# First loads of a fused attention and FFN kernel: nine transfers on one DMA queue instead of two, and four warm-up matmuls fewer

## The chip, the core and the metric

The kernel runs on one NeuronCore of a Trainium2 chip. The metric is the device time of one execution in microseconds. TensorE (PE) multiplies matrices, with its weight loads shown apart as PEld; VectorE (DVE), ScalarE (ACT) and GpSimd (POOL) work on elements; SyncE (SP) only issues DMAs here. ACT can issue DMAs as well. An instruction that issues a DMA occupies its engine's sequencer for a while; the transfer itself runs on 16 DMA engines and raises a semaphore when it has landed.

## The reference

One input x of 2048 tokens by 640 features goes through two branches, and a gate per token mixes them. Everything is bf16.

```
x = A_x                                          # 1 x 2048 x 640
g = sigmoid((x * gate_w).sum(-1))                # one gate per token
q, k, v = split(x @ wqkv)                        # 32 heads of 20
phi(t) = [softmax(t @ w_phi), softmax(-t @ w_phi)]   # 40 features per head
kv = sum over tokens of phi(k)^T v;  z = sum over tokens of phi(k)
a = (phi(q) kv) / (phi(q) z + 1e-6) @ wo
b = (silu(x @ w_gate) * (x @ w_up)) @ w_down     # hidden width 1728
out = g * a + (1 - g) * b
```

## The kernel before

Tokens are worked in 16 tiles of 128 (number t), features in 5 chunks of 128 (number c). Almost every matmul needs x transposed, with features on the partitions: the tile xT holds it. Tiles 0 to 3 are loaded as they are into xs (`load_x`, items x0 to x3) and transposed by TensorE (`xpose`, items X0 to X3, line 306, with a copy from PSUM to xT on DVE, line 318). Tiles 4 to 15 come through DMA transposes (`load_xt`, items t4 to t15, line 347).

Two lists written out by hand fix the order of everything. `LOADS` is the order in which DMAs are issued:

```
x0 w0 x1 w1 x2 w2 x3 w3 w4 f0 h k0 k1 t4 k2 k3 k4 t5 t6 t7 t8 t9 t10 t11 t12 t13 t14 t15 q0 q1 q2 q3
q4 f1 f2
```

- x0 to x3: x of tiles 0 to 3, 128x640 each. The list `XQ` gives the engine whose queue each is issued on: x0 on SP, x1, x2 and x3 on ACT.
- w0 to w4: the five chunks of the V columns of wqkv, into wvg, 128x640 each. `WQ` puts w0 to w3 on SP and w4 on ACT.
- f0, f1, f2: parts of w_gate and w_up (wg and wu), f0 the first 256 columns of each. h: w_phi (wph).
- k0 to k4: the K columns of wqkv, transposed on the way into wT. q0 to q4: the same for the Q columns. All of f, h, k, t and q are on SP.

A small load of gate_w (gwr) stands ahead of all on ACT. Each engine keeps its own instructions in the order in which they are written, so SP and ACT each run through their share of this list.

`ORDER` is the order of the compute items. The stretch of TensorE that matters here is:

```
H0 .. H8 H12 G X0 H9 H10 U0.0 X1 H11 U1.0 U0.1 U1.1 X2 U2.0 U0.2 U1.2 U2.1 X3 U2.2 U0.3 ...
U2.4 V3 Y F0.1 M1 i3 M0 F0.0 M2 V4 M3 M4 K0 K1 I S0 V6 V5 ...
```

- H (`warm`, line 472): two dummy matmuls of 128x128 on constants. Nothing uses their result. G: gate_w, transposed into a column of wvg.
- Ut.c (`vpart`): V of tile t, the part of chunk c, two matmuls of 320 columns each (line 294), as soon as wvg chunk c and xT of tile t are there. V3, V4 ...: V of a whole tile, ten matmuls.
- F0.1, F0.0: two of the 14 FFN items of the first 512 tokens, ten matmuls of 512 columns each, with wg and wu of f0.
- Y (`w_blocks`): w_phi spread into block-diagonal form (wbd) by POOL and DVE. Mm (`premult`): chunk m of the K weights, multiplied with w_phi ahead of use, from wT chunk m (item km) and wbd.
- K, S, P, E: K projections with exponentials, sums, normalising, and the sums kv. Q, A, B, C, c, O, D later: the same for Q, the output and the final products.

Waits are made by a tracker (`_Tracker.run`): each instruction waits for the semaphores of what it reads and overwrites. Every DMA has a semaphore of its own. PSUM banks are used in pairs, the least recently used first (`next_pair`), so an item that is taken out also moves which pair the following ones use.

Of the kernel before, what the change touches and what calls it, by code (L numbers as in the profile page):

```python
# [6 lines left out]
P = 128  # L7
S_TOK = 2048
D = 640
# [24 lines left out]
"""  # L34

ORDER = """
H0 H1 H2 H3 H4 H5 H6 H7 H8 H12 G X0 H9 H10 U0.0 X1 H11 U1.0 U0.1 U1.1 X2 U2.0 U0.2 U1.2 U2.1
X3 U2.2 U0.3 U1.3 U2.3 U0.4 U1.4 U2.4 V3 Y F0.1 M1 i3 M0 F0.0 M2 V4 M3 M4 K0 K1 I S0 V6 V5 S1 P0
K3 K2 P1 E0 V9 K4 E1 S3 V7 P3 K5 S2 V8 V10 S4 P2 P4 E2 R0 E3 K6 S5 P5 S6 i4 E4 V14 K7 K8 P6 V15 S7
R2 E5 K9 S8 P7 R1 E6 K10 S9 V12 P8 E7 P9 K11 S10 P10 F0.2 R3 F1.2 E8 E9 K12 E10 S11 S12 K14 S14  # L40
# [11 lines left out]
class _Tracker:  # L52
# [90 lines left out]
    def run(self, eng, fn, reads=(), writes=(), dma=False):  # L143
        rkeys = list(dict.fromkeys(k for a in reads for k in self.keys_of(a)))
        wkeys = list(dict.fromkeys(k for a in writes for k in self.keys_of(a)))
        need = {}

        def req(ev, raw):
            if ev is None:
                return  # L150
            s, v = ev
            if s == eng and not dma and (eng == "pe" or not raw):
                return
            if v > need.get(s, 0):
                need[s] = v

        for k in rkeys:
            for kk in self._conflicts(k):
                req(self.lastw[kk], True)
                if k[0] == "psum":  # L160
                    for s, v in self.readers[kk].items():
                        req((s, v), False)
        for k in wkeys:
            for kk in self._conflicts(k):
                req(self.lastw[kk], True)
                for s, v in self.readers[kk].items():
                    req((s, v), False)
        self._wait(eng, need)
        ins = fn()
        if dma:  # L170
            sn = "d%d" % self.ndma
            self.ndma += 1
            self._add_sem(sn)
            inc = 16
        else:
            sn, inc = eng, 1
        ins.then_inc(self.sem[sn], inc)
        self.cnt[sn] += inc
        v = self.cnt[sn]
        snap = dict(self.known[eng])  # L180
        if not dma:
            snap[sn] = max(snap.get(sn, 0), v)
        self.evknow.setdefault(sn, {})[v] = snap
        ev = (sn, v)
        for k in wkeys:
            self.lastw[k] = ev
            self.readers[k] = {}
        for k in rkeys:
            r = self.readers[k]
            if r.get(sn, 0) < v:  # L190
                r[sn] = v
        return ev


def _build(nc, A_x, A_wqkv, A_w_phi, A_wo, B_x, B_w_gate, B_w_up, B_w_down, gate_w, out):
    tr = _Tracker(nc)
    pe, act, dve, pool, sp = nc.tensor, nc.scalar, nc.vector, nc.gpsimd, nc.sync
# [3 lines left out]
    def sb(name, shape, dtype):  # L201
        t = nc.alloc_sbuf_tensor(name, list(shape), dtype)
        tr.reg(t, "sbuf", nc.lookup_mloc(t).addr)
        return t
# [3 lines left out]
    wvg = sb("wvg", [P, 5, D + 2], BF16)  # L208
# [42 lines left out]
    def at(name, shape, dtype, rel):  # L251
        n = mybir.dt.size(dtype)
        for s in shape[1:]:
            n *= s
        assert rel + n <= SLAB, (name, rel + n, SLAB)
        t = nc.alloc_sbuf_tensor_at(name, list(shape), dtype, offset=sbase + rel)
        tr.reg(t, "sbuf", sbase + rel)
        return t
# [4 lines left out]
    xs = at("xs", [P, NPE, D], BF16, 10752)  # L263
# [78 lines left out]
    def dma(e, dst, src, transpose=False):  # L342
        eo = tr.eng[e]

        def fn():
            if transpose:
                return eo.dma_start_transpose(dst, src)
            return eo.dma_start(dst, src)
        rd = [src] if src.tensor.name in tr.base else []
        wr = [dst] if dst.tensor.name in tr.base else []  # L350
        return run(e, fn, rd, wr, dma=True)
# [4 lines left out]
            channel_multiplier=cm), [ap], [ap])  # L356


    XQ = ["sp", "act", "act", "act"]
    WQ = ["sp", "sp", "sp", "sp", "act"]  # L360
    x2 = A_x[0]
    out2 = out[0]

    def load_rows(e, dst, c, c0):
        dma(e, dst, A_wqkv[c * P:(c + 1) * P, c0:c0 + D])

    def load_x(t):
        dma(XQ[t], xs[:, t, :], x2[t * P:(t + 1) * P, :])

    def load_xt(t):  # L370
        dma("sp", xT[:, t, :, :], x2[t * P:(t + 1) * P, :], transpose=True)
# [3 lines left out]
        dma("sp", wu[:, :, c0:c1], B_w_up[:, c0:c1].rearrange("(c p) j -> p c j", p=P))  # L375

    def load_wv(c):
        load_rows(WQ[c], wvg[:, c, 0:D], c, 2 * D)

    dma("act", gwr[0:5, :], bass.AP(gate_w.tensor, gate_w.offset, [[P, 5], [1, P]]))  # L380

# [13 lines left out]
    H0 = [0, 6, 12, 19, 25]  # L395
    H1 = [7, 13, 20, 26, 32]
# [339 lines left out]
    def kv_end():  # L736
# [4 lines left out]
        "H": lambda i: warm(), "i": fills, "X": xpose, "G": gcol, "U": vpart, "V": vtile,  # L741
        "M": lambda m: premult(1, m), "R": lambda m: premult(0, m),
        "K": ktile, "S": knorm, "P": kmul, "p": lambda t: kmul(t, "dve"), "E": kvtile, "x": load_x, "t": load_xt, "w": load_wv, "h": load_phi, "k": lambda m: load_wt(1, m), "q": lambda m: load_wt(0, m),
        "f": lambda i: load_ffn(FCUT[i], FCUT[i + 1]), "L": load_late_weights, "T": tail_weights, "J": gates,
        "Y": w_blocks, "I": kv_begin, "N": kv_end, "Z": z_row,
# [8 lines left out]
def bass_gated_mix__linear_kernel_hedgehog__swiglu_ffn__prompt_kernel(  # L754
    nc: bass.Bass,
    A_x: bass.AP,
    A_wqkv: bass.AP,
    A_w_phi: bass.AP,
    A_wo: bass.AP,
    B_x: bass.AP,  # L760
    B_w_gate: bass.AP,
    B_w_up: bass.AP,
    B_w_down: bass.AP,
    gate_w: bass.AP,
    out: bass.AP,
):
    _build(nc, A_x, A_wqkv, A_w_phi, A_wo, B_x, B_w_gate, B_w_up, B_w_down, gate_w, out)
# [28 lines left out]
```

The softmax here doesn't subtract the row's maximum and nothing guards it: scores larger than these inputs give would overflow.

## Time and profile before

| | |
|---|---|
| median of 4 runs | 289.41 us (289.14 to 290.11) |
| profiled execution | 289.17 us, span in the profile 287.9 us |
| PE busy | 285.0 us, 99% of the span |
| PEld busy | 174.7 us, 61% |
| DVE, ACT, POOL busy | 162.6, 148.1, 160.4 us |
| DMA on SP's queue (q1) | 48190 packets, 20.62 MB |
| DMA on ACT's queue (q10) | 730 packets, 0.68 MB |
| granted TensorE clock | 1.0 |

A line of the timeline reads: start in us, length in us, engine, line of the kernel, operation, tile written <- tiles read, shape, count, and in brackets how long the engine stood idle before it and what released it. SPq and ACTq are the DMA-issuing instructions of those engines: the length is that of the issue, not of the transfer. The landing time of a transfer is counted from the start of its issue. The chain lists the work that ended last, followed back from the end. Matmuls are pipelined and their ends are modelled, so PE looks busy in short waits too; the weight loads (PEld) show these better.

### The profile page before, as it was taken

Reading aid. Unit: us, or ns where it says so; the run is one execution under the profiler, and the core shown is the slowest. Engines: PE = TensorE matmul, PEld = TensorE weight load, DVE = VectorE, ACT = ScalarE, POOL = GpSimd, SP = SyncE. Lnnn points to the kernel's source line nnn. Section 1 sums busy time; section 2 is a strip of 40 time slices with the busy share of each in tenths; the row PEclk is TensorE's granted clock in tenths of the full one; section 3 lists DMA queues with packets and bytes.
Section 4 is the critical chain, followed back from the end, with each engine's and each line's share of the span. In section 5 each row is a group of like instructions: output and inputs, shape, how many; then the busy total and the mean of one; then the engine's idle time right before and its main releaser. Section 6 shows DMA issues by size and latency. Waiting matters only on the chain.

```text
span 287.9 us, 4897 instructions
## 1 busy us (share of the span) xinstructions
PE 285.0 (99%) x1975; PEld 174.7 (61%) x1975; DVE 162.6 (56%) x243; ACT 148.1 (51%) x252; POOL 160.4 (56%) x125
## 2 busy tenths in 40 slices
PE   8999999999999999999999999999999999999997
PEld 6667777575644545557775556675554446656776
DVE  2147748486468987679992385970317799200000
ACT  1478778676775555673445663225575452234112
POOL 8286899789445789835643348350753649601000
PEclk9999999999999999999999999999999999999999
DMA  7987589000010497302293002061020004410101
GB/s 217 174 121 127 102 220 359 14 1 2 2 47 0 100 310 144 69 2 50 50 149 88 10 1 50 2 147 44 2 50 0 2 1 87 89 46 0 49 23 48
DMA packets 48943, 21.62 MB, mean 75 GB/s; under 512 B 39384, under 2 KB 48792, under 8 KB 48920
## 3 DMA queue, kind: packets, MB, share of 16 engines
q1 hardware_dynamic: 48190, 20.62, 31.7%
q10 hardware_dynamic: 730, 0.68, 0.7%
q8 instruction: 16, 0.26, 0.4%
q14 instruction: 7, 0.06, 0.1%
HBM read 9.29 MB, written 2.62 MB: 41 GB/s over the span
## 4 chain that ended last, share of the span: by engine, by line
PE 99%; DVE 0%; issue 0%
PE ps L294 97%; PE ps L472 1%; PE ps L306 1%; DVE osb L724 0%; DVE xT L318 0%
## 5 line engine op out<-in xcount | busy, mean ns | idle before, releaser
L322 POOL TENSOR_TENSOR hT<-hT,us 128x512 bf16<-128x512 bf16 (+1 forms) x56 | 65.6, 1181 | 66.3 <-DVE hT L326 66.0
L326 DVE SCALAR_TENSOR_TENSOR hT<-hT,ps 128x512 bf16<-128x512 bf16 (+1 forms) x56 | 37.6, 684 | 72.9 <-ACT hT L312 60.6
L294 PE MATMUL ps<-xT,wg 128*128 128x512 bf16 x260 | 64.6, 379 | 0.0
L294 PE MATMUL ps<-xT,wu 128*128 128x512 bf16 x260 | 64.6, 379 | 0.0
L294 PE MATMUL ps<-wd,hT 128*128 128x320 bf16 (+2 forms) x462 | 63.9, 295 | 0.0
L312 ACT ACTIVATE hT<-ps 128x512 bf16<-128x512 f32 (+2 forms) x60 | 35.8, 596 | 46.6 <-PE ps L294 46.4
L322 POOL TENSOR_TENSOR ph<-eq,qc 128x1320 bf16<-128x1320 bf16 x16 | 42.3, 2645 | 26.1 <-DVE qc L632 24.0
L294 PEld LDWEIGHTS ps<-wd,hT 128*128 128x128 bf16 x462 | 44.5, 98 | 17.5 <-issue 0.2
L294 PE MATMUL ps<-wqk,xT 128*128 128x320 bf16 x320 | 47.7, 299 | 0.1
L294 PEld LDWEIGHTS ps<-xT,wu 128*128 128x128 bf16 x260 | 25.4, 98 | 30.7
L294 PEld LDWEIGHTS ps<-xT,wg 128*128 128x128 bf16 x260 | 25.0, 98 | 27.8 <-ACT oT L312 0.8
L312 ACT ACTIVATE osb<-ps,omg 128x640 bf16<-128x640 f32 (+2 forms) x17 | 12.9, 758 | 53.7 <-PE ps L294 53.7
L322 POOL TENSOR_TENSOR ekr<-ekr,krec 128x1280 bf16<-128x1280 bf16 x16 | 37.4, 2357 | 4.9 <-DVE krec L336 4.9
L294 PEld LDWEIGHTS ps<-wqk,xT 128*128 128x128 bf16 x320 | 30.5, 98 | 13.2 <-ACT us L312 0.5
L312 ACT ACTIVATE us<-ps 128x512 bf16<-128x512 f32 (+1 forms) x56 | 33.2, 593 | 0.3 <-POOL hT L322 0.2
L312 ACT ACTIVATE eq<-ps 128x640 bf16<-128x640 f32 x32 | 22.4, 704 | 17.3 <-POOL ph L322 10.4
L333 DVE TENSOR_REDUCE ksum<-ekr 128x64 f32<-128x1280 bf16 x16 | 23.5, 1470 | 10.7 <-ACT ekr L312 10.7
L312 ACT ACTIVATE ekr<-ps 128x640 bf16<-128x640 f32 x32 | 22.3, 704 | 8.2 <-PE ps L294 7.7
L333 DVE TENSOR_REDUCE qz<-eq 128x64 f32<-128x1280 bf16 x16 | 23.7, 1479 | 2.2 <-ACT eq L312 2.2
L294 PE MATMUL ps<-wog,oT 128*128 128x320 bf16 (+2 forms) x165 | 24.7, 294 | 0.0
L294 PE MATMUL ps<-wvg,xT 128*128 128x320 bf16 (+1 forms) x160 | 24.6, 301 | 0.1
L333 DVE TENSOR_REDUCE qw<-ez 128x64 f32<-128x1280 bf16 x16 | 23.6, 1478 | 0.0
(73 smaller groups left out, 188.5 us busy)
## 6 DMA issues: line engine op xcount, KB each, us to landing
out_dram<-osb SPq DMA_DIRECT2D x15, 160.0 KB, 1.9
wd<-in_B_w_down_dram SPq DMA_DIRECT2D x1, 2080.0 KB, 10.6
wg<-in_B_w_gate_dram SPq DMA_DIRECT2D x1, 1040.0 KB, 10.9
wu<-in_B_w_up_dram SPq DMA_DIRECT2D x1, 1040.0 KB, 10.8
wg<-in_B_w_gate_dram SPq DMA_DIRECT2D x1, 800.0 KB, 7.1
wu<-in_B_w_up_dram SPq DMA_DIRECT2D x1, 800.0 KB, 8.6
wog<-in_A_wo_dram SPq DMA_DIRECT2D x2, 375.0 KB, 7.2
wvg<-in_A_wqkv_dram SPq DMA_DIRECT2D x4, 160.0 KB, 3.9
```

Of the source, the lines that this page charges most:

```text
L294: last = pe.matmul(o, lhsT=l, rhs=r, start=st, stop=sp_, skip_group_check=sk)
L306: last = pe.transpose(o, i, ident[0:k, 0:k])
L312: return run("act", lambda: act.activation(o, i, func, scale=scale), rd, [o])
L322: return run(e, lambda: eo.tensor_tensor(o, a, b, op), [a, b], [o])
L326: return run("dve", lambda: dve.scalar_tensor_tensor(out=o, in0=a, scalar=s, in1=b, op0=op0, op1=op1), rd, [o])
L333: return run("dve", lambda: dve.tensor_reduce(o, i, AX.X, ALU.add), [i], [o])
L472: last = pe.matmul(bank(2 * pr, 0, P), lhsT=c, rhs=c, start=True, stop=True)
```

## The change

All nine loads of x0 to x3 and w0 to w4 are issued on SP's queue, in the order of `LOADS`: x0 w0 x1 w1 x2 w2 x3 w3 w4. ACT's queue keeps only gwr (and one store at the end). Two of the `warm` items between the first transposes go: H10, after X0, and H11, after X1, two dummy matmuls each. One `warm` item, H9, stays there. Nothing else is moved in either list.

```
 ORDER = """
-H0 H1 H2 H3 H4 H5 H6 H7 H8 H12 G X0 H9 H10 U0.0 X1 H11 U1.0 U0.1 U1.1 X2 U2.0 U0.2 U1.2 U2.1
+H0 H1 H2 H3 H4 H5 H6 H7 H8 H12 G X0 H9 U0.0 X1 U1.0 U0.1 U1.1 X2 U2.0 U0.2 U1.2 U2.1
...
-    XQ = ["sp", "act", "act", "act"]
-    WQ = ["sp", "sp", "sp", "sp", "act"]
...
     def load_x(t):
-        dma(XQ[t], xs[:, t, :], x2[t * P:(t + 1) * P, :])
+        dma("sp", xs[:, t, :], x2[t * P:(t + 1) * P, :])
...
     def load_wv(c):
-        load_rows(WQ[c], wvg[:, c, 0:D], c, 2 * D)
+        load_rows("sp", wvg[:, c, 0:D], c, 2 * D)
```

## The prediction

> **What bounds the kernel now.** I read the page's chain first, then the same chain in order of time, then the timeline of the first 20 us on TensorE's weight loads, VectorE and the two DMA queues, and last the landing times of single transfers. The chain says that TensorE sets the end:
>
> ```profile
> PE 99%; DVE 0%; issue 0%
> PE ps L294 97%; PE ps L472 1%; PE ps L306 1%; DVE osb L724 0%; DVE xT L318 0%
> ```
>
> In order of time it shows where TensorE is not free-running:
>
> ```profile
> 5.42 0.93 PE ps L294 x6
> 6.35 0.07 PE ps L306
> 6.42 0.02 issue
> 6.44 0.24 DVE xT L318
> 6.68 0.05 issue
> 6.73 1.27 PE ps L294 x8
> 8.00 0.28 PE ps L306 x5
> 8.28 8.24 PE ps L294 x56
> 16.52 0.03 issue
> 16.55 61.33 PE ps L294 x584
> ```
>
> From 16.55 us on TensorE is dense to the end (its weight-load queue idles 3 us in the remaining 271, all far later and none of it for the loads that move). So a change in the first 16 us counts as far as it moves that 16.55. A busy PE hides small waits, so I use the weight loads' idle time:
>
> ```profile
> 6.72 0.94 PEld L294 LDWEIGHTS ps<-wvg,xT 128*128 128x128 bf16 x8 [0.27 <-DVE xT L318]
> ...
> 16.55 0.31 PEld L294 LDWEIGHTS ps<-wbd,wT 128*128 128x128 bf16 x6 [0.52 <-DMA wT<-in_A_wqkv_dram]
> ```
>
> The second line is premult M2: TensorE has stood 0.52 us for wT block k2, a DMA transpose on SP's queue. Its tile view gives k2 issued at 11.61 and landed 4.9 us later, at 16.5. **That transfer, not the x and wv loads, is the last wait before the dense stretch.** What sets k2's issue is SP's queue:
>
> ```profile
> 0.80 0.39 SPq L348 DMA_DIRECT2D xs<-in_A_x_dram  x1
> 1.25 1.84 SPq L348 DMA_DIRECT2D wvg<-in_A_wqkv_dram  x4
> 3.14 0.43 SPq L348 DMA_DIRECT2D wg<-in_B_w_gate_dram  x1
> 3.62 0.53 SPq L348 DMA_DIRECT2D wu<-in_B_w_up_dram  x1
> 4.19 0.59 SPq L348 DMA_DIRECT2D wph<-in_A_w_phi_dram  x1
> 4.82 5.43 SPq L347 DMA_TRANSPOSE wT<-in_A_wqkv_dram  x2
> 10.29 1.28 SPq L347 DMA_TRANSPOSE xT<-in_A_x_dram  x1
> 11.61 4.28 SPq L347 DMA_TRANSPOSE wT<-in_A_wqkv_dram  x3
> ```
>
> A transpose issue takes 1.28 us, but the tile view gives k0's 4.12 us (4.82 to 8.94); from k1 (8.98) on they follow each 1.31 us: t4 10.29, k2 11.61.
>
> **What the Trainium skill says.** (1) "DMA: Bandwidth & Descriptors", section "Issuing engines are not separate DMA queues": SP's and ACT's transfers share the same 16 engines, and issuing from both saves only issue time. (2) Same page, "Queues, rings and completion order": each engine takes turns between the queues it has work for. The trace agrees with both: from 4 to 6 us ACT's queue (q10) and SP's (q1) hold about half each of a full 16 engines:
>
> ```profile
> DMA packets 581, 0.66 MB, mean 332 GB/s; under 512 B 63, under 2 KB 581, under 8 KB 581
> ...
> q1 hardware_dynamic: 285, 0.33, 53.8%
> q10 hardware_dynamic: 296, 0.34, 47.3%
> ```
>
> (3) "TensorE: Matmul & The Clock Gate", "What's actually happening": the clock is halved until about 3.4 us of sustained activity. The page's clock row shows full speed from the start, but the 20 first dummies need 2.06 us of weight loads, 0.103 each, and the V matmuls after 8 us run at 0.133 each for 320 columns; per column that is 0.80 against 0.41 ns. I believe the durations: TensorE warms up between 4.2 and 5.3 us.
>
> **The change part by part.**
>
> *Three x loads and w4 go to SP.* Thirteen issues stand in SP's list before k1 where there were nine. At 0.46 us each (wvg: 1.84 for 4), x0, w0, x1, w1, x2, w2, x3, w3, w4 start at 0.80, 1.25, 1.71, 2.17, 2.62, 3.08, 3.54, 3.99, 4.45, and wg, wu, wph, k0 at 4.9, 5.4, 6.0, 6.6: four issues, 1.8 us later than before. ACT is freed of four issues (1.39 to 3.20); it waits for POOL until 5.01 in any case, so that is worth nothing.
>
> *When they land.* The engines are 80 to 108% busy from 2 us on in both kernels, so I let the same bytes flow in the new order. Summing the GB/s of half-microsecond windows of before: 164 KB by 2.65, 328 by 3.25, 491 by 3.8, 655 by 4.3, 819 by 4.75, 983 by 5.2. x0 landed at 3.0, some 0.4 after its bytes. With that lag: w0 3.65, x1 4.2, w1 4.7, x2 5.15, w2 5.6, x3 6.1, w3 6.7, w4 7.3. Before, by issue plus landing time: w0 4.05, x1 4.4, w1 5.3, x2 6.0, w2 6.4, x3 6.6, w3 8.2, w4 8.45. Each of the nine is sooner or equal; supply is not short, since 164 KB per 0.46 us is 356 GB/s against a drain of 200 to 370.
>
> *TensorE's start with that.* Before: U0.0 4.20 (w0), X1 4.49 (x1), U1.0/U0.1 5.35 (w1), X2 6.05 (x2), U2.0 6.72 (VectorE's copy), X3 7.70, then 24 V matmuls without a wait from 8.06 to 11.24. After: X0 3.18 to 3.6, two dummies, VectorE's copy at 3.73, so U0.0 at 3.85; X1 4.2 (x1); its first copy waits for VectorE (busy with x0's until 4.35) and X1, so U1.0 at 4.8, U0.1 and U1.1 to 5.6; X2 5.6 (x2 is there); copy, U2.0 at 6.2; four parts of 0.26; X3 7.25; 24 matmuls from 7.6. **Gain at this point 0.45 us.**
>
> *Four dummies go* (H10, H11: 4 x 0.07 to 0.12 us, 0.4 at most). They stood in the waits for w0 and w1; the gain above already has them out. Costed at 0 beyond it, with the clock as a risk below.
>
> *What stands next.* F0.1 comes at 10.8; wu landed at 10.5 before. Its bytes and those before it are the same, so about 10.5 again: no wait, or one of some tenths that the next one covers. M1 needs POOL's wbd (12.28) and k1, at 13.0: covered. F0.0 ends, and TensorE is ready for M2 at 16.02 - 0.45 = 15.6 in place of 16.02.
>
> *k2.* No row shows k0's issue behind four more loads. From below: nothing stalls, k0 takes 1.28 from 6.6, ends at 7.9, and the chain of transposes is 1.06 us earlier. From above: its 4.12 us belong to k0 itself and count from 6.6: 1.8 us later. I take the middle: k0's issue stood until the queue ahead had drained to a point near the end of wg (landed 9.4); wg, wu and wph stand directly ahead of k0 in both kernels, and the bytes ahead of that point are the same. Other issues support a full queue as the cause: a plain load of wg stands 2.73 us at 39.31 behind queued transposes and weights. So k0 ends at about 8.9 +/- 0.3, and k2 lands at 16.5 +/- 0.3. M2's wait grows from 0.52 to about 0.95 and **takes the whole gain**.
>
> *Queued behind.* V4, M3, M4, K0, K1, V6 follow M2 on TensorE. t4 and k4 (17.7, used at about 18.5) have 0.8 us or more; t6 lands at 21.3 for V6 at 21.46, 0.2 us. If the chain moves, t6 and k2 move together, so V6 adds nothing; t9 has 3 us.
>
> Sum: -0.45 (V stage) + 0.45 (M2's wait), with a tenth in favour of the denser queue. The profiled execution took 289.17 with a span of 287.9, 0.24 below the median of 289.41. Against the median: **289.3 us**.
>
> **The rivals.**
>
> *No change (0.42).* As above: 288.9 to 289.9.
>
> *Faster (0.26): the transposes come earlier too.* For it: a single queue moved 335 to 369 GB/s near 41 us, while the two gave only 243 to 257 from 5.5 to 6.5; and k2's 4.9 us contain a stretch (15 to 16 us) of under 50 GB/s that need not recur, the later transposes landing in 2.9 to 4.7. Against: the four runs before lie within 1 us, so such stretches look systematic. If k2 is there by 15.6, TensorE's order decides and all of 0.95 us is gained: 288.4.
>
> *Slower (0.24): SP's issue order is the price.* k2 and t6 have no slack worth naming, so every microsecond by which the four inserted issues delay k1 is paid in full. If k0's long issue is its own and not the queue's, M2 waits until 18.3: +1.8, 291.2. It decides from a chain that is later at all; half the shift gives 290.3. Against it: the stalled plain load named above, and transposes at 15.9 to 27 us that issue in 1.28.
>
> *The clock warms later (0.08).* With four fewer dummies TensorE could stay at half speed until 7.5: the V work of that time, about 1.5 us, is doubled, TensorE reaches M2 at 17.1, +0.5: 289.9. Against: the real work moves into the same place.
>
> That the change does nothing on the queue can't be: SP's list in the changed program is x0, w0, x1, w1, x2, w2, x3, w3, w4.
>
> **How the numbers follow.** What a measurement of this kernel tells from no change is about 0.3%, 0.87 us. Faster than 288.54 is most of the second case, 0.24. Slower than 290.28 is most of the third and a tail of the fourth, 0.26. The rest is 0.50. The range takes the full gain, 288.4, and most of the way to the full delay, 290.9; the likeliest case alone would be 288.9 to 289.9.
>
> **What would show it.** Right: X2's weight loads near 5.6, the 24 V matmuls from about 7.6, M2's idle before it near 0.95 and still put down to wT, k1's issue at 8.7 to 9.3. Wrong: k1 near 7.9 and no wait at M2 (second case); k1 after 9.8 (third); 0.23 us or more per V matmul after 6 us (fourth).

## The result and the profile after

The changed kernel takes 290.69 us (median of 43 executions, 289.51 to 293.07), the kernel before 289.61 in the same comparison. The ratio is 1.0035, with a 95% interval of 1.0023 to 1.0046: **slower by 1.0 us**. The profiled execution of the changed kernel took 290.57 us, with a span of 289.3; before it was 289.17 and 287.9.

The chain on the page of the changed kernel, by engine and by line:

```profile
PE 92%; SPq 5%; DMA 2%; issue 0%; DVE 0%
PE ps L294 92%; SPq L347 3%; SPq L348 2%; DMA wT<-in_A_wqkv_dram 2%; DVE osb L722 0%; PE ps L306 0%
```

Before, TensorE held 99%. Now the chain leaves TensorE for the first 20 us and runs through SP's queue. In order of time, it runs back from the dense stretch to a single transpose:

```profile
15.20 0.04 issue
15.24 4.64 DMA wT<-in_A_wqkv_dram
19.88 0.05 issue
19.93 59.32 PE ps L294 x562
```

That transfer is k4, the last K block, 4.64 us from its issue to its landing. SP's timeline shows why it was issued at 15.24 (14.3 before):

```profile
4.09 0.91 SPq L348 DMA_DIRECT2D wvg<-in_A_wqkv_dram  x2
5.04 0.43 SPq L348 DMA_DIRECT2D wg<-in_B_w_gate_dram  x1
5.51 0.53 SPq L348 DMA_DIRECT2D wu<-in_B_w_up_dram  x1
6.08 0.87 SPq L348 DMA_DIRECT2D wph<-in_A_w_phi_dram  x1
7.00 4.23 SPq L347 DMA_TRANSPOSE wT<-in_A_wqkv_dram  x2
11.28 1.29 SPq L347 DMA_TRANSPOSE xT<-in_A_x_dram  x1
12.60 3.92 SPq L347 DMA_TRANSPOSE wT<-in_A_wqkv_dram  x3
```

k0's issue starts at 7.00, 2.2 us later than before, but takes 2.92 us (tile view) in place of 4.12. It ends at 9.92, 1.0 us later, and k1, t4, k2, k3 and k4 behind it are each issued 1.0 us later. TensorE's weight loads show what that does:

```profile
4.84 0.28 PEld L306 LDWEIGHTS ps<-ident,xs 128*128 128x128 bf16 x5 [0.78 <-DMA xs<-in_A_x_dram]
...
8.10 3.18 PEld L294 LDWEIGHTS ps<-wvg,xT 128*128 128x128 bf16 x24
...
16.36 0.33 PEld L294 LDWEIGHTS ps<-wbd,wT 128*128 128x128 bf16 x6 [0.29 <-DMA wT<-in_A_wqkv_dram]
...
19.93 0.31 PEld L294 LDWEIGHTS ps<-wbd,wT 128*128 128x128 bf16 x6 [1.55 <-DMA wT<-in_A_wqkv_dram]
```

X1 waits 0.78 us for x1, but the 24 V matmuls start at 8.10 against 8.06, so the V stage lost nothing in this execution and gained nothing. M2 waits 0.29 us (0.52 before). The new wait is M4's, 1.55 us for k4; against M2's 0.23 us less, it accounts for about all of the 1.4 us by which the span grew (289.3 less 287.9).

That k4 also took 1.2 us longer to land (4.6 us, before 3.4) goes with a pause in the transfers. These are windows of half a microsecond; the last two columns are the DMA share and GB/s. After:

```profile
18.50:19.00 0.50, 0.07 (x2) 0.00 (x0) 0.40 (x1) 0.50 (x2) 0.50 (x2) 1.00 2.53 73
19.00:19.50 0.50, 0.00 (x0) 0.00 (x0) 0.43 (x1) 0.05 (x1) 0.50 (x2) 1.00 0.18 13
```

Before, such a pause stood while k2 was under way:

```profile
15.00:15.50 0.50, 0.50 (x5) 0.20 (x3) 0.50 (x2) 0.45 (x1) 0.33 (x1) 1.00 2.31 41
15.50:16.00 0.50, 0.50 (x4) 0.26 (x3) 0.32 (x1) 0.00 (x0) 0.50 (x1) 1.00 0.08 9
```

Other profiles have it at other times (8 GB/s from 15.0 us in d_only, 11 from 16.5 in chain_late, 10 from 18.5 in a_k2first). Which block it meets bears on which premult waits, so the sizes of the single waits belong to one execution each.

Why the issues are late shows in what the DMA engines moved at the start. Before:

```profile
4.00:4.50 0.50, 0.50 (x5) 0.20 (x4) 0.36 (x1) 0.00 (x0) 0.50 (x1) 1.00 0.97 356
4.50:5.00 0.50, 0.50 (x5) 0.38 (x4) 0.00 (x0) 0.00 (x0) 0.50 (x2) 1.00 1.02 369
```

After:

```profile
4.00:4.50 0.50, 0.48 (x4) 0.06 (x1) 0.36 (x1) 0.00 (x0) 0.50 (x1) 1.00 0.99 274
4.50:5.00 0.50, 0.16 (x3) 0.16 (x4) 0.00 (x0) 0.00 (x0) 0.50 (x2) 1.00 0.94 269
```

The engines hold packets 94 to 102% of the time in both, yet move a quarter less. It is not that every packet takes longer: the median packet of 1280 bytes takes 55 ns in both. From 4 to 5 us, 11 of the changed kernel's 238 packets took over 0.11 us, the longest 0.63, and filled a quarter of the engines' time; of the 313 before none took over 0.08. From 4 to 6 us the changed kernel has one queue at work:

```profile
DMA packets 489, 0.56 MB, mean 279 GB/s; under 512 B 54, under 2 KB 489, under 8 KB 489
...
q1 hardware_dynamic: 489, 0.56, 97.7%
```

Issue plus landing time: x1 4.8, w1 5.3, x2 5.9, w2 6.6, x3 7.1, w3 7.7, w4 8.8, wg 10.3, wu 11.3. Before, wg was there at 9.4 and wu at 10.5.

### The profile page after: what moved, and what is told of

It reads as the page before. It is cut to its first block, busy times and chain, and to the rows that moved or that the text cites. A ratio compares the mean times of both kernels' runs of the same rounds, so it can differ in the third digit from the quotient of the medians.

```text
span 289.3 us, 4890 instructions
## 1 busy us (share of the span) xinstructions
PE 284.6 (98%) x1971; PEld 174.3 (60%) x1971; DVE 162.6 (56%) x243; ACT 148.2 (51%) x252; POOL 160.4 (55%) x125
## 4 chain that ended last, share of the span: by engine, by line
PE 92%; SPq 5%; DMA 2%; issue 0%; DVE 0%
PE ps L294 92%; SPq L347 3%; SPq L348 2%; DMA wT<-in_A_wqkv_dram 2%; DVE osb L722 0%; PE ps L306 0%
## 5 line engine op out<-in xcount | busy, mean ns | idle before, releaser
L312 ACT ACTIVATE eq<-ps 128x640 bf16<-128x640 f32 x32 | 22.4, 704 | 17.3 <-POOL ph L322 10.4
```

The costliest lines, as they stand in the source:

```text
L312: return run("act", lambda: act.activation(o, i, func, scale=scale), rd, [o])
```

## The experiments

Each is compared with the kernel before on the same chip. A ratio of 1.001 is 0.29 us.

**The two parts apart: q_only and d_only.**

```
q_only: the changed kernel, with  X0 H9 H10 U0.0 X1 H11 U1.0  in ORDER
d_only: the kernel before, with   X0 H9 U0.0 X1 U1.0          in ORDER
```

> The queue part alone: all nine loads on SP's queue, the four dummies H10 and H11 kept. Ring theory (SP's queue alone drains the x and wv loads more slowly than the two queues together, so k0 and every transpose behind it come later): as the changed kernel, k1 issued near 9.96 us, about +1.0 us against before (ratio 1.003 to 1.004). Issue theory (the four more issues in SP's list, 0.46 us each, push k0 back): the same. Dummy theory (TensorE's clock or bank order suffers from the four dummies that are gone): as before, within 0.3 us.

> The dummy part alone: H10 and H11 out, the loads on two queues as before. Ring theory and issue theory: k1 at 8.98 us as before, the time within 0.3 us of before, if anything a little less. Dummy theory: about +1.0 us (ratio 1.003 or more), and V matmuls at over 0.2 us each after 5.4 us.

q_only: ratio 1.0026 (1.0012 to 1.0039), some +0.75 us, k1 issued at 10.3. d_only: 1.0012 (0.9990 to 1.0033), not resolved, k1 at 8.6. In q_only's profile TensorE waits for k2 and for k4:

```profile
16.90 0.31 PEld L294 LDWEIGHTS ps<-wbd,wT 128*128 128x128 bf16 x6 [0.73 <-DMA wT<-in_A_wqkv_dram]
19.76 0.31 PEld L294 LDWEIGHTS ps<-wbd,wT 128*128 128x128 bf16 x6 [0.86 <-DMA wT<-in_A_wqkv_dram]
```

The queue part by itself costs time. The dummies' share is not resolved: the interval of their own run reaches from -0.3 to +1.0 us.

**Four more issues without their data: small4.**

```
 LOADS: ... x3 w3 w4 s0 s1 s2 s3 f0 h k0 ...       (kernel before otherwise)
+def load_small(i):
+    dma("sp", scr[:, i, :], x2[i * P:(i + 1) * P, 0:32])
```

> Before, with four extra loads of 128x32 elements (8 KB each, into a tile that nobody reads) on SP's queue between w4 and f0: four issues more in SP's list and 512 descriptors more, but only 32 KB of data. ACT keeps x1, x2, x3, w4. Issue theory: k0 starts 1.8 us later and k1 moves from 8.98 to about 10 us, +1.0 us as in the changed kernel. Ring theory: ACT's queue still fills the engines, k1 within 0.3 us of 8.98, time within 0.3 us of before.

Ratio 0.9997 (0.9982 to 1.0012): no cost. SP's list is as late as in the changed kernel:

```profile
3.14 1.85 SPq L348 DMA_DIRECT2D scr<-in_A_x_dram  x4
...
6.89 3.73 SPq L347 DMA_TRANSPOSE wT<-in_A_wqkv_dram  x2
```

k0 starts at 6.89, almost as in the changed kernel, but k1 follows at 9.4, 0.4 us after before, and the engines move 359 GB/s from 4 to 6 us. SP's time for four issues is therefore not the price; k0 waits for the queue to drain either way. It is the draining that is slower in the changed kernel. k4 was even issued as late as there (15.26), but it landed in 3.4 us, at 18.7, and TensorE lost about 0.1 us at M3 and M4. A late issue of k4 alone is thus not the whole price; its landing counts too.

**The order of use on two queues: alt.** The lists against those of before; H10 and H11 are out as in the changed kernel.

```
-XQ = ["sp", "act", "act", "act"]            +XQ = ["sp", "sp", "sp", "sp"]
-WQ = ["sp", "sp", "sp", "sp", "act"]        +WQ = ["act", "act", "act", "act", "act"]
```

> The order of use kept, but on two queues: x0 to x3 on SP, w0 to w4 on ACT (behind gwr), dummies as in the changed kernel. SP has four of the nine issues ahead of wg where before has five. Ring theory: the engines move 320 GB/s or more from 3 to 6 us as before, k1 at 8.98 us or up to 0.4 us sooner, time -0.5 to +0.1 us against before. Issue theory: k0 starts 0.46 us sooner than before and k1 moves by as much, to 8.5 us, time -0.4 us. If what costs is the order of use and not the single queue: k1 near 9.96 us, +1.0 us.

Ratio 1.0044 (1.0026 to 1.0062), +1.3 us: a miss for both theories. The third case on record, that the order of use costs (k1 near 9.96, +1.0), comes nearest, but f1first below moves the same order fast. k1 was issued at 9.6, and only 257 GB/s moved from 4 to 6 us although both queues had work. The loss in its profile is another one, though. w1 landed at 6.8 (5.4 before), and TensorE stood for it in the V stage:

```profile
6.83 0.39 PEld L294 LDWEIGHTS ps<-wvg,xT 128*128 128x128 bf16 x4 [1.17 <-DMA wvg<-in_A_wqkv_dram]
```

Here x2, x3 and wg on SP's queue take turns with w1 and w2 on ACT's, and the order of use is lost between the queues. M2 (at 17.34) and M4 then wait for no wT block. That one queue alone is the cause of the slow draining can't be upheld after this run.

**Is one queue slow? merged and f1first.** Both are made from the changed kernel.

```
merged:  LOADS  x0 w0 x1 w1.2 x2.2 w3.2 f0 h ...     (w1+w2, x2+x3, w3+w4 in one transfer each)
f1first: LOADS  f1 x0 w0 x1 w1 x2 w2 x3 w3 w4 f0 h ...
```

> The changed kernel with six transfers in place of nine on SP's one queue, the same bytes in nearly the same order: x0, w0, x1, w1+w2, x2+x3, w3+w4. The last x or wv load is issued by 3.1 us in place of 4.6, and wg near 3.6 in place of 5.0. Pace theory (one engine issues 164 KB each 0.47 us, about what the 16 DMA engines move, so there is never a stock of queued work; an engine that stalls once is late for good, others run dry): with larger transfers a stock builds up, 320 GB/s or more from 3.5 to 6.5 us, k1 at 9.2 us or sooner in place of 9.96, the time within 0.4 us of before. Ring theory (one queue's ring alone moves only 260 to 280 GB/s, however much is queued): k1 still after 9.7 us, about +0.8 us against before.

> A measurement of one queue with work in stock: the changed kernel with f1 (wg and wu columns 256 to 896, 1.64 MB) issued ahead of x0 on SP's queue. It is slower by 4 to 6 us, since every x and wv load waits behind f1; its time is not the question. When f1 has drained near 6.5 us all nine x and wv loads are queued in the same ring. Pace theory: they then follow each other at the engines' rate, 0.44 to 0.48 us from one median landing to the next, 330 GB/s or more. Ring theory, or a gap at the end of each small transfer: 0.55 to 0.65 us each and 250 to 290 GB/s, as in the changed kernel, where they landed some 0.6 us apart.

f1first is the clearest result of the study. The nine small transfers, queued behind f1's two large ones in the same queue, landed at 8.1, 8.5, 8.9, 9.3, 9.7, 10.2, 10.6, 11.0 and 11.5 us, 0.42 us apart; in the changed kernel they took 0.71 us each (3.1 to 8.8). The windows of f1first:

```profile
8.00:8.50 0.50, 0.34 (x4) 0.35 (x5) 0.02 (x1) 0.00 (x0) 0.00 (x0) 1.00 1.06 387
8.50:9.00 0.50, 0.50 (x7) 0.50 (x5) 0.30 (x2) 0.00 (x0) 0.00 (x0) 1.00 1.07 392
9.00:9.50 0.50, 0.50 (x4) 0.27 (x3) 0.34 (x1) 0.00 (x0) 0.00 (x0) 1.00 1.08 394
```

One queue moves 390 GB/s of the very same loads when they wait in it, and from 4 to 6 us, with f1's data, it moved 386, so the time since the start is not what slows a single queue. The ring theory and a cost at the end of each transfer fall. What is left on record is that the changed kernel lacks queued work, since SP issues 164 KB each 0.47 us, 350 GB/s at best; what speaks against that stands under the open questions. f1first's one execution took 295.49 us, +5.8.

merged agrees at most in part: with six issues, k1 came at 9.3 and 311 GB/s moved from 4 to 6 us, but from 3.5 to 6.5 us, the stretch for which I had asked 320, it was 289. The ratio of 1.0023 (1.0010 to 1.0037) is +0.7 us, outside the 0.4 us that I expected. Its profile has no wait for a wT block at all, but another loss:

```profile
5.39 0.45 PEld L306 LDWEIGHTS ps<-ident,xs 128*128 128x128 bf16 x5 [1.33 <-DMA xs<-in_A_x_dram]
...
7.31 0.74 PEld L306 LDWEIGHTS ps<-ident,xs 128*128 128x128 bf16 x5
```

X1 waited 1.33 us, and X2's five weight loads took 0.74 us in place of 0.40: TensorE was at half speed until after 9 us, where it is at full speed from about 5 in the profiles of before and after. Its span was 290.1. This opened the question that the last three runs are about.

**Which transpose counts: a_k2first and b_k2first.** k2 ahead of t4 in LOADS, in the changed kernel and in the one before: `h k0 k1 k2 t4 k3 k4`.

> The changed kernel with k2 ahead of t4 in the list of loads; nothing else moved. If the late chain of transposes is what costs, and its last member that TensorE waits for is k4 (M4 waited 1.55 us in the profile of the changed kernel, M2 only 0.29): M2's wait goes, but M4 waits for k4 by so much longer, and the time stays within 0.3 us of the changed kernel (+0.8 to +1.2 us against before). If M2's k2 is what sets the time, as I had it in the prediction: 0.3 us or more is won back against the changed kernel.

> The kernel before with k2 ahead of t4. In its profile M2 waited 0.52 us for k2, which would now be issued at 10.3 in place of 11.6 us, and t4 has 3 us to spare. If k2 is the last wait there: 0.3 to 0.5 us less than before (ratio 0.9983 to 0.999). If k4 or t6 takes its place (they had 0.8 and 0.2 us to spare): 0.0 to 0.2 us less.

a_k2first: 1.0024 (1.0014 to 1.0034), +0.7 us. That lies between the two cases on record, so the time does not decide between them. In the profile M2's wait goes and M4 waits:

```profile
19.53 0.31 PEld L294 LDWEIGHTS ps<-wbd,wT 128*128 128x128 bf16 x6 [1.00 <-DMA wT<-in_A_wqkv_dram]
```

b_k2first: 1.0001 (0.9985 to 1.0018). Taking M2's wait away in the kernel before is worth nothing measurable; in its profile TensorE waits for no wT block any more, and w0 and x1 came later than in the profile of before (4.8 and 5.0 us for 4.1 and 4.4), so that M2 was reached no sooner (16.56 us).

**The chain late by itself: chain_late.** The kernel before with two small loads between k0 and k1: `h k0 s0 s1 k1 t4`.

> The kernel before with two extra small loads (128x32 elements each, into a tile that nobody reads) on SP's queue between the transposes k0 and k1; all x, wv, wg, wu and wph loads and the dummies as before. That delays k1 and every transpose behind it by two issues, about 0.93 us (k1 from 8.98 to 9.9 us), and nothing ahead of it. If the late chain is by itself what the change costs: TensorE waits for k2 and k4 by 0.7 to 1.5 us more, +0.6 to +1.1 us against before, as in the changed kernel (+1.0). If the later x and wv loads or the V stage cost it: within 0.2 us of before.

Ratio 1.0020 (1.0010 to 1.0030), +0.6 us, with all loads ahead of k1 untouched. k1 came at 10.11, k4 landed at 19.9 as in the changed kernel. So the later chain by itself costs 0.3 to 0.9 us in the median. The profiled execution is no witness for the wait at M2 or M4: it was another with TensorE at half speed until some 9 us (X2's loads again 0.74 us), and M2 came at 18.19 when k2 had been there since 17.3.

**The chain made early again: a_f0act and b_f0act.**

```
 def load_ffn(c0, c1):
+    if c0 == 0: tr._wait("act", dict([xev[1]]))     # a_f0act alone: after x1
-    dma("sp", wg...) ; dma("sp", wu...)             and wph in load_phi
+    dma("act", wg...) ; dma("act", wu...)           f0 alone; f1 and f2 stay on SP
```

> The changed kernel with wg, wu (f0) and wph issued on ACT's queue, where they wait for x1 to have landed (about 4.8 us); SP goes from w4 straight to k0, which starts near 5.0 in place of 7.0 us with no wg, wu, wph ahead of it in its ring. Chain theory: k1 well before 9 us, no wait at M2 or M4, and the loss of the change is won back: -0.3 to +0.2 us against before, unless wu now lands after 11.4 us and F0.1 waits for it instead (each tenth is paid). If the chain were not the cause: still +0.8 to +1.1 us.

> The kernel before with wg, wu (f0) and wph on ACT's queue behind w4 (no added wait); SP goes from w3 to k0, which starts near 3.2 in place of 4.8 us. The chain of transposes should be 1.5 us or more earlier than before, so M2's 0.52 us and its neighbours' waits go: 0.2 to 0.5 us less than before if wu still lands by 11.3 us. The transposes now share the engines with wg and wu: if wu lands at 12 us, F0.1 waits 0.7 us and the gain is gone or turned into +0.3 us.

a_f0act: 1.0042 (1.0015 to 1.0068). The chain was early (k1 at 7.1, k4 landed at 17.2) and no wait for wT is left. But the transposes and wg now run beside w3 and w4, which landed at 10.4 and 12.0:

```profile
10.41 0.66 PEld L294 LDWEIGHTS ps<-wvg,xT 128*128 128x128 bf16 x6 [2.13 <-DMA wvg<-in_A_wqkv_dram]
12.02 2.04 PEld L294 LDWEIGHTS ps<-wvg,xT 128*128 128x128 bf16 x16 [0.95 <-DMA wvg<-in_A_wqkv_dram]
```

The loss has only moved. I had looked for it at wu. b_f0act: 1.0008 (0.9996 to 1.0021), no gain: k4 comes 1.4 us sooner, wu at 11.6 and w1 at 6.2 later. What one transfer gained another lost.

**The dummies and the clock: a_warm, b_warm, b_nodum.**

```
a_warm (changed kernel): X0 H9 H10 U0.0 H11 H13 H14 H15 X1 H16 U1.0
b_warm (kernel before):  X0 H9 H10 H13 U0.0 H14 X1 H11 U1.0
b_nodum (kernel before): X0 U0.0 X1 U1.0
```

> The changed kernel with dummies back where TensorE waits: two more before U0.0, eight between U0.0 and X1 (the 0.78 us in which it stood for x1) and two after X1. Two profiles (merged, chain_late) show TensorE still at half speed until 8.5 us where the others are at full speed from about 5: X2's five weight loads took 0.74 us in place of 0.40, and the V work came 2 us later. Clock theory: the change makes such executions more frequent; with the waits filled they go, and 0.4 us or more of the +1.0 us is won back. Chain theory alone: the chain of transposes is as late as in the changed kernel, M2 and M4 wait as there, +0.8 to +1.1 us against before.

> The kernel before with two more dummies before U0.0 and two between U0.0 and X1, where it waits for w0 and x1; loads as before. They cost TensorE at most 0.4 us, which M2's wait for k2 (0.52 us) covers. Clock theory: the executions of before above 290.6 us (12 of 64 in the first comparison) are those with the late clock, and become fewer: median 0.0 to 0.3 us less than before. Otherwise: within 0.2 us of before.

> The kernel before without any dummy between the first transposes (H9, H10, H11 all out, six matmuls), loads as before. Clock theory: the late clock comes in most executions, +1.0 to +2.0 us against before, and if the profile is such a one, X2's five weight loads take 0.74 us and F0.1 starts at 13.3 us or later. If the dummies there don't matter: within 0.3 us of before, as with two of three out (+0.3, not resolved).

b_nodum: 1.0030 (1.0013 to 1.0047). Its executions fall in two groups, ten from 288.8 to 290.6 us and ten from 291.1 to 292.1; one more took 1710 us, which I can't explain. The profile shows the late clock without any late load:

```profile
4.75 0.74 PEld L306 LDWEIGHTS ps<-ident,xs 128*128 128x128 bf16 x5
...
6.96 0.74 PEld L306 LDWEIGHTS ps<-ident,xs 128*128 128x128 bf16 x5
...
9.28 0.40 PEld L306 LDWEIGHTS ps<-ident,xs 128*128 128x128 bf16 x5
```

k2 landed at 14.9 there and was not waited for; F0.1 started at 12.86 (11.28 before), and this execution took 290.55 us, 1.4 more than the profiled one of before. So leaving all three items out costs time, and the profile shows one way: the clock comes late. They are no full guard, since chain_late's profile has the late clock with all of them in place. The upper group is longer still, and whether the late clock is what sets it apart is not shown, for lack of a profile from it. a_warm: 1.0031 (1.0021 to 1.0042). Filling the waits won back nothing that can be measured, where the clock theory asked for 0.4 us; k1 came at 10.0 and k4 landed at 19.3. But its profile does not show the waits of the chain theory either:

```profile
6.96 0.40 PEld L306 LDWEIGHTS ps<-ident,xs 128*128 128x128 bf16 x5
...
17.05 0.51 PEld L294 LDWEIGHTS ps<-wbd,wT 128*128 128x128 bf16 x6
18.83 0.88 PEld L294 LDWEIGHTS ps<-wbd,wT 128*128 128x128 bf16 x12
```

x1 landed at 5.2, X2 came at 6.96 (6.09 in the changed kernel), and by the time TensorE reached M2, M3 and M4, the late blocks were there or nearly there. The V stage was late by about as much as the chain, and the run does not separate the two. b_warm: 1.0006 (0.9995 to 1.0016), no gain; none of its 14 executions is above 290.3 us. Its X2 came at 6.61 (6.05 before), so the dummies' own time may have taken back what that is worth.

No version here is measurably faster than the kernel before.

## Why the prediction was wrong, point by point

I forecast 289.3 us and no change; it is 1.0 us slower, the side to which I gave 0.26. The median lies inside the range that I gave.

*What bounds the kernel* held: TensorE is dense after the premults, and their wT blocks on SP's queue are the last wait. b_k2first adds a limit to it: M2's 0.52 us of the profile was worth nothing in the median.

*When they land* is **the step that failed**, in two terms. The first is the rate: I let the same bytes flow at the rate of before in the new order. Between 3.5 and 5.5 us 213 to 300 GB/s moved in place of 318 to 369, and the nine loads' worth of bytes, 1.47 MB, had moved by 7.5 us where my working has 6.9. (Nor were the engines 80% busy throughout: from 6.0 to 6.5 us they were at 73% before and 71% after.) The second is the lag of 0.4 us between bytes and landing, which I took from x0. A load has landed when the last of the 16 engines has delivered its share. 0.49 MB had moved by 3.75 us, as I had it, and the median engine had delivered x1 at 3.98, but the last only at 4.80; for w4 these were 7.85 and 8.76. So x1 came at 4.8 (I said 4.2), w4 at 8.8 (7.3), wg at 10.3 (as before, 9.4).

Of the 13 profiles in which the nine loads stand in one of these two arrangements, the eight with them split as before moved 302 to 359 GB/s from 4 to 6 us; the five with all nine on SP's queue moved 257 to 281. The Trainium skill's sentence that I leaned on ("DMA: Bandwidth & Descriptors", "Issuing engines are not separate DMA queues") says that a second issuing engine saves only issue time, usually small beside the transfer. Here one issue takes 0.47 us, as long as its 164 KB at 350 GB/s, and putting these loads on one queue cost 0.75 us (q_only). That the issue time is the reason is not shown: alt kept two issuing engines and cost 1.3 us.

*TensorE's start*: the gain of 0.45 us rested on these landing times and is absent: 8.10 in place of 7.6.

*k2*: the mechanism was right, its date was not. k0's issue ended 0.5 us ahead of wg's landing before, and 0.4 us ahead of it after, and 0.2 to 0.5 us ahead in all 14 profiles in which it stands behind wph: it is released as the queue drains to wg, whenever it started (4.82, 6.89 in small4, and 7.00 where I had 6.6). My 8.9 +/- 0.3 took the drain for unchanged; it was 9.92.

*Queued behind*: I gave k4 0.8 us to spare and moved on. A chain 1.0 us later and a landing 1.2 us slower (4.6 against 3.4 us) use that up, and M4 waits 1.55 us. The slower landing goes with a pause like the one that I had seen in k2's 4.9 us and weighed for k2 alone; this time it passed k2 (3.7 us) and met k4. M2, on which I had all eyes, waits less than before.

*The dummies*: costed at nothing (and at 0.07 to 0.12 us each, four are up to 0.5 us, not 0.4). These four alone are not resolved (d_only); all six out cost 0.9 us (b_nodum, 1.0030), so that nothing was the lower bound.

*The rivals*. The slower one had the direction, and its half shift of 290.3 us lies near the 290.69 measured. That the loss equals k1's delay of 1.0 us is in part chance: in small4 k1 came 0.4 us and k4's issue 1.0 us later, and nothing was lost. Its place, M2 and t6, was not where the largest wait stood, and its reason, that k0's long issue belongs to k0, was wrong, as small4 shows. The late clock is real, at 1.4 us in the execution of b_nodum that shows it and not the 0.5 us that I gave it, but the profiled execution of the changed kernel does not have it (X2's weight loads 0.40 us).

*What stays open.* Why the x and wv loads drain more slowly in the new arrangement. Missing stock fits f1first, and merged in part. Three things speak against it. alt had work on both queues and moved 257 GB/s. In the changed kernel all x, wv, wg and wu loads, 2.13 MB, had been issued by 6.04 us and 1.09 MB had moved by 6, yet from 6.5 to 9 us it moved 279 GB/s (before 315). And engines without work would stand idle, where the windows from 4 to 5 us show them occupied, a quarter of the time by a few long packets. What makes those packets long no run shows. Open too is how often the late clock comes in the changed kernel: it can't be read from its executions, because the two losses overlap. With one profile to a kernel, the share of each in the median of 1.0 us is not known.

## What to carry to other kernels

Where a list of loads is moved to one queue, the order of arrival is not the only thing that changes: the rate may change too, so read the GB/s of short windows, not the busy share, and reckon with the last engine that delivers, not with the mean. A queue of transposes behind those loads is released when they have drained, so follow the last member that anything waits for, not the first. Where two stages stand within 1 us of each other, as the V stage and the transposes do here, a wait that is taken out of one tends to be found in the other. And before taking out dummy matmuls in a wait, look at the durations after it: an execution that loses the clock there pays more (1.4 us here) than the dummies cost (some 0.1 us each).

## What the runs showed of the hardware

- One queue moved 384 to 394 GB/s of the x and wv loads, nearly all in 1280-byte packets, when they stood behind f1 (f1first, 8 to 10 us), and 386 of f1 itself from 4 to 6 us. With the same loads at the head of the queue it moved 257 to 281 from 4 to 6 us (five profiles).
- A lower rate can come from a few long packets while the others keep their pace: the median packet of 1280 bytes took 55 ns in all 16 profiles from 4 to 6 us, but in the changed kernel 11 of 238 filled a quarter of the engines' time.
- A load lands with the last of the 16 engines, here up to 0.9 us after the median one (w4: 7.85 and 8.76 us).
- The transposes' transfers have pauses: half a microsecond with 8 to 13 GB/s, from 15.0 us in d_only, 15.5 before, 16.5 in chain_late, 18.5 in a_k2first and 19.0 after.
- The half-speed clock does not show in the granted clock, which reads 1.00 in every window of b_nodum's and merged's profiles. Only the durations tell: 0.74 us for five transposes' weight loads at half speed, 0.40 at full speed. X2's took 0.40 in twelve profiles (from 5.97 us on) and 0.74 in merged, chain_late and b_nodum (from 6.96 on), where X3's were the first with 0.40, from 9.28 to 10.05. That agrees with "TensorE: Matmul & The Clock Gate", "What's actually happening", in the Trainium skill: the clock is opened by a busy window of about 3.4 us, one of a row of windows that runs freely. From it I infer that an execution that misses one has to wait for the next; no run shows the windows themselves.
- A transpose issue of 1.28 us can stand for 2.4 to 4.8 us (small4 and alt), and how long depends on the data ahead of it, not on the instructions: k0's ended between 8.2 and 9.3 us in the seven profiles with split loads and k0 behind wph, though it started between 4.8 and 6.9.
